# Starting the projections of a segment-recurrent transformer earlier: halved first Q weights, second x chunk by the ACT queue, roots on ScalarE, warm-up matmuls and interleaved transposes

## The chip, the cores and the metric

The kernel runs on one core of one Trainium2 chip. The metric is the device time of one execution in microseconds (us). Most executions of this kernel lie within 0.3% of each other; here that is about 2.6 us.

## The reference

Only the first half matters here. A layer-normed x of 2048 rows by 512 is cut into 64 segments of 32 rows. Each segment is joined with 8 rows of memory that the segment before it computed; 32 heads of 128 attend over these 40 rows, and the output projection gives the next memory. So the segments are a chain. A gated MLP follows.

```python
for s in range(n_seg):                       # 64 segments, one after the other
    xs = x[:, s*32:(s+1)*32, :]
    h = concatenate([mem, xs], axis=1)       # 8 memory rows + 32 rows
    q = einsum('btd,dhe->bhte', h, Wq)       # Wq, Wk, Wv: 512 x 32 x 128, 4 MB each
    k = einsum('btd,dhe->bhte', h, Wk)
    v = einsum('btd,dhe->bhte', h, Wv)
    p = softmax(where(mask, q @ k.T * scale, -1e9))
    o = einsum('bhte,hed->btd', p @ v, Wo)
    mem = o[:, :8]                           # feeds segment s+1
    outs.append(o[:, 8:])
# then h2 = h + gated MLP of layernorm(h)
```

## The kernel before

The kernel records operations for the five engines; a small emitter works out from the tokens that each operation reads and writes which semaphores it must wait for. Every engine then runs its own list in order. The queries, keys and values of the 32 rows of a segment do not depend on the memory. The kernel computes those of its last 8 rows (the "x chunks" below, 16 segments each) apart from the rest, and for chunks 0 and 1 ahead of the loop over segments: Q groups, then V of chunk 0, half of the K groups, V of chunk 1, the other K groups. This start is what the change touches. (`...` marks cuts.)

```python
def load_xe(ck, j):
    t, tok = xbuf(j)
    sp(lambda e: e.dma_start(t, xe[CK*ck:CK*ck+CK, XM:SEG, :]), writes=tok)
def load_w(mi, hq):                          # 8 heads of one matrix: 1 MB
    ...
    sp(lambda e: e.dma_start(ws[:, :, c0:c1], wr[:, :, c0:c1]), writes=[("W", mi, hq)])

load_xe(0, 0)                                # all on the SP queue, in order
load_xe(1, 1)
for hq in range(4): load_w(0, hq)            # Wq
...
def ln_stats(j):                             # mean and variance on VectorE, root on GpSimd
    dve(... bn_stats ...); dve(... bn_aggr ...)
    pool(... var + EPS ...); pool(... ** -0.5 ...)
def qkx_mm(ck, i, bank):                     # one group: 16 matmuls of 128x128x128
    for hh in range(4):
        for dc in range(DC):
            pe(... matmul(ps[:, bank, ...], lhsT=ws[:, dc, ...], rhs=hTe[:, ck % 3, dc, :]) ...)
...
for j in range(2): ln_stats(j)
for j in range(2):
    ln_apply(j); xT(j, 6 + j); xe_copy(j, 6 + j)     # transpose on TensorE, copy on ScalarE
for mi in (2, 1):                            # Wv, then Wk
    for hq in range(4): load_w(mi, hq)
for i in range(8):                           # Q groups, 2 of each weight quarter per chunk
    for ck in range(2): start_group(qkx_mm, qkx_evac, ck, i)
    ...
for n in range(8):                           # V of chunk 0
    ...
    start_v(0, n)
    if n == 1: xT(4, 6); ring_copy(0, 6)
    if n == 2: xT(5, 7); ring_copy(1, 7)
    if n == 3: xT(6, 6); xe_copy(2, 6); mem0_transpose(7); load_wo(0)
load_wo(1)
for j in range(2): load_vx(j)                # reads stored V back
for i in range(8, 12):                       # first K groups
    for ck in range(2): start_group(qkx_mm, qkx_evac, ck, i)
for n in range(8):                           # V of chunk 1
    start_v(1, n)
    if n % 4 == 3: load_wo(2 + n // 4)
for i in range(12, 16): ...                  # last K groups
...
for s in range(NSEG): ...                    # the loop over segments
```

The softmax here doesn't subtract the row's maximum and nothing guards it: scores larger than these inputs give would overflow.

## Time and profile before

| | us |
|---|---|
| time before, median of 3 runs (870.05 to 871.07) | 870.4 |
| span in the profile | 869.6 |
| TensorE busy | 848.4 (98%) |
| first Q matmul | 8.01 |
| first K group | 33.65 |
| first matmul of the loop over segments | 55.17 |

The page of the kernel before: its span, the busy time of the engines, and the first line of the chain of work that ended last.

```profile
span 869.6 us, 45456 instructions
...
PE 848.4 (98%) x22453; PEld 433.6 (50%) x18876; DVE 502.0 (58%) x1246; ACT 467.4 (54%) x1291; POOL 158.6 (18%) x427
...
PE 96%; DVE 2%; DMA 1%; issue 1%; ACT 0%; POOL 0%; SPq 0%; DVEq 0%
...
```

TensorE is nearly always busy and makes up 96% of that chain. A change of the start can therefore gain only what it moves the loop forward.

The timeline of the first 14 us. Columns: start in us, duration, engine, line of the source, operation, output<-input, and in brackets the idle time of the engine before it and what ended that.

```profile
...
2.16 2.67 SPq L315 DMA_DIRECT2D f_arena<-in_A_Wq_dram  x4
...
5.17 0.69 DVE L364 BATCH_NORM_STATS2 f_st<-f_xn 128x6 f32<-128x512 bf16 x1 [0.82 <-DMA f_xn<-in_A_x_dram]
...
5.99 0.38 DVE L374 TENSOR_SCALAR f_xn<-f_xn,f_mv,f_rs 128x512 bf16<-128x512 bf16 x1
...
6.43 0.61 PE L384 MATMUL f_ps<-f_ident,f_xn 128*128 128x128 bf16 x4 [6.43 <-DVE f_xn L374]
...
9.96 0.74 ACT L436 ACTIVATE f_arena<-f_ps 128x512 bf16<-128x512 f32 x1 [1.11 <-PE f_ps L426]
11.67 0.73 DVE L438 CAST f_arena<-f_ps 128x512 bf16<-128x512 f32 x1 [4.12 <-PE f_ps L426]
13.06 0.75 ACT L436 ACTIVATE f_arena<-f_ps 128x512 bf16<-128x512 f32 x1 [2.36 <-PE f_ps L426]
13.95 0.74 DVE L438 CAST f_arena<-f_ps 128x512 bf16<-128x512 f32 x1 [1.55 <-PE f_ps L426]
```

VectorE waits for the second x chunk (5.17) before it normalizes the first (5.99). After the Q matmuls begin, the evacuations of the first groups start 9.96, 11.67, 13.06, 13.95: a group of 16 matmuls takes 1.71 us at first and 0.89 us later, 107 and 56 ns per matmul. The Trainium skill ("TensorE: Matmul & The Clock Gate", Part 1) gives 106.7 and 55.6 ns for a cold and a warm array, and this trace agrees. The trace's clock record begins with an entry of 1.0 at 12.54 us; that is where the spacing changes.

TensorE alone, from the timeline: the Q groups, the V groups, the first K groups, the loop.

```profile
...
8.01 16.62 PE L426 MATMUL f_ps<-f_hTe,f_arena 128*128 128x128 bf16 x256
24.57 1.91 PE L461 MATMUL f_ps<-f_arena,f_hTe 128*32 128x512 bf16 x32
...
30.08 3.64 PE L461 MATMUL f_ps<-f_arena,f_hTe 128*32 128x512 bf16 x64
33.65 7.32 PE L426 MATMUL f_ps<-f_hTe,f_arena 128*128 128x128 bf16 x128
...
55.17 0.40 PE L280 MATMUL f_ps<-f_arena,f_hT 128*32 128x512 bf16 x4
...
```

Each load is confirmed by 16 DMA engines, and the trace has the time of each confirmation. I call the last of the 16 the landing. The first 1 MB of Wq landed at 7.76; the first piece of Wk landed at 31.79, although 14 of its engines were through by 30.63.

```profile
...
q8 instruction: 164, 2.69, 1.4%
...
```

The columns are packets, MB and share of the 16 engines. 2.69 MB in 164 packets is 16.4 KB each. TensorE runs 22,453 matmuls and 18,876 weight loads, 252 per packet. The Trainium skill ("Advanced Engine Details and Errata", ISA Cache) gives a line of 16 KB, 256 instructions; this agrees. Nearly all of this queue is TensorE's instruction stream.

### The profile page before, as it was taken

The page shows a single profiled execution, that of the slowest core. Times are in us where ns is not written, and L with a number is a line of the kernel's source. Part 1 is how long each engine was busy: PE and PEld are TensorE (multiplying, and loading weights), DVE is VectorE, ACT ScalarE, POOL GpSimd, SP SyncE. Part 2 cuts the span into 40 slices and gives each one's busy share as a digit, 9 for nine tenths or more (in the row PEclk, how much of TensorE's full clock was granted, in tenths as well). Part 3 has the DMA queues.
Part 4 walks back from the last instruction along what each step waited for, and adds up shares of the span by engine and source line. Part 5 has one row for each costly group of instructions (what it writes and reads, how often), then busy time and mean ns, then how long its engine had stood idle before and what let it go on. Part 6 is the DMA issues. An engine that isn't in the chain of part 4 may idle for free.

```text
span 869.6 us, 45456 instructions
## 1 busy us (share of the span) xinstructions
PE 848.4 (98%) x22453; PEld 433.6 (50%) x18876; DVE 502.0 (58%) x1246; ACT 467.4 (54%) x1291; POOL 158.6 (18%) x427
## 2 busy tenths in 40 slices
PE   6999999999999999999999999999999999999996
PEld 6664445554444545454454544545544444444443
DVE  3546666666666666666666666566565554454343
ACT  3445666666666666656666666666666655300000
POOL 1621212121122112121212212121111122100000
PEclk9999999999999999999999999999999999999999
DMA  9972333214041222332241313333221790033001
GB/s 319 380 218 72 72 71 74 65 41 81 29 91 33 75 39 52 76 67 62 68 85 40 79 50 83 70 80 71 47 67 38 200 267 1 0 109 110 25 19 33
DMA packets 114183, 75.23 MB, mean 87 GB/s; under 512 B 70712, under 2 KB 99520, under 8 KB 113984
## 3 DMA queue, kind: packets, MB, share of 16 engines
q1 hardware_dynamic: 113984, 72.26, 30.8%
q8 instruction: 164, 2.69, 1.4%
q14 instruction: 35, 0.29, 0.1%
HBM read 39.46 MB, written 20.58 MB: 69 GB/s over the span
## 4 chain that ended last, share of the span: by engine, by line
PE 96%; DVE 2%; DMA 1%; issue 1%; ACT 0%; POOL 0%; SPq 0%; DVEq 0%
PE f_ps L280 30%; PE f_ps L660 13%; PE f_ps L281 13%; PE f_ps L1092 11%; PE f_ps L426 3%; PE f_ps L710 3%; PE f_ps L461 3%; PE f_ps L1054 3%; PE f_ps L574 3%; PE f_ps L625 3%; PE f_ps L1085 3%; PE f_ps L1166 2%; PE f_ps L631 1%; PE f_ps L554 1%; PE f_ps L681 1%
## 5 line engine op out<-in xcount | busy, mean ns | idle before, releaser
L280 PE MATMUL f_ps<-f_arena,f_hT 128*32 128x512 bf16 (+1 forms) x5120 | 352.7, 337 | 1.6 <-issue 0.5
L281 PE MATMUL f_ps<-f_arena,f_hT 128*32 128x256 bf16 (+1 forms) x3072 | 214.4, 308 | 0.0
L280 PEld LDWEIGHTS f_ps<-f_arena,f_hT 128*32 128x32 bf16 x5120 | 121.1, 96 | 168.5 <-issue 85.2
L518 ACT ACTIVATE f_Tst<-f_ps 128x512 bf16<-128x512 f32 (+1 forms) x320 | 149.8, 510 | 57.6 <-PE f_ps L280 53.9
L660 PE MATMUL f_ps<-f_arena,f_cT 128*32 128x256 bf16 x4096 | 133.9, 273 | 1.2 <-ACT f_cT L645 1.1
L597 POOL TENSOR_TENSOR f_E_sb<-f_R_sb,f_E_sb 128x64 bf16<-128x64 f32 x128 | 48.2, 377 | 378.7 <-ACT f_R_sb L589 378.7
L526 DVE STREAM_TRANSPOSE f_QT<-f_Tst 128x256 uint32<-128x256 uint32 x128 | 57.1, 446 | 94.9 <-ACT f_Tst L518 94.9
L660 PEld LDWEIGHTS f_ps<-f_arena,f_cT 128*32 128x32 bf16 x4096 | 92.4, 95 | 34.9 <-ACT f_cT L645 21.1
L1092 PE MATMUL f_ps<-f_arena 128*128 128x512 bf16 x448 | 100.6, 379 | 0.0
L617 DVE TENSOR_SCALAR f_V_sb<-f_ps 128x512 bf16<-128x512 f32 (+1 forms) x128 | 70.6, 552 | 41.1 <-PE f_ps L280 41.1
L672 ACT ACTIVATE f_part<-f_ps 128x256 bf16<-128x256 f32 x128 | 49.2, 384 | 67.4 <-PE f_ps L660 67.4
L647 DVE TENSOR_SCALAR f_cT<-f_ps 128x160 bf16<-128x160 f32 (+1 forms) x192 | 61.0, 374 | 38.3 <-PE f_ps L631 38.3
L645 ACT ACTIVATE f_cT<-f_ps 128x160 bf16<-128x160 f32 (+1 forms) x192 | 53.0, 348 | 39.4 <-PE f_ps L631 39.4
L1092 PEld LDWEIGHTS f_ps<-f_arena 128*128 128x128 bf16 x448 | 43.8, 98 | 52.7
L526 DVE STREAM_TRANSPOSE f_KT<-f_Tst 128x128 uint32<-128x128 uint32 (+1 forms) x192 | 66.0, 356 | 2.7
L585 ACT ACTIVATE f_R_sb<-f_ps 128x160 f32<-128x160 f32 x128 | 38.9, 304 | 33.6 <-PE f_ps L281 26.4
L1098 DVE TENSOR_TENSOR f_arena<-f_ps,f_arena 128x512 f32<-128x512 f32 x28 | 19.3, 690 | 54.4 <-PE f_ps L1092 52.4
L567 ACT ACTIVATE f_E_sb<-f_ps 128x224 bf16<-128x224 f32 x128 | 45.7, 357 | 0.1
L593 DVE TENSOR_TENSOR f_E_sb<-f_R_sb,f_E_sb 128x160 bf16<-128x160 f32 x128 | 44.8, 350 | 0.0
L589 ACT ACTIVATE f_R_sb<-f_R_sb 128x160 f32<-128x160 f32 x128 | 42.6, 333 | 2.0
L710 PE MATMUL f_ps<-f_arena,f_cTx 128*32 128x512 bf16 x512 | 40.5, 380 | 0.0
L280 PE MATMUL f_ps<-f_arena,f_hTe 128*32 128x512 bf16 x512 | 39.0, 382 | 0.0
(105 smaller groups left out, 1026.0 us busy)
## 6 DMA issues: line engine op xcount, KB each, us to landing
wT_d<-f_wst SPq DMA_DIRECT2D x32, 256.0 KB, 2.9
f_arena<-wT_d SPq DMA_DIRECT2D x32, 256.0 KB, 4.2
f_arena<-in_A_Wq_dram SPq DMA_DIRECT2D x4, 1024.0 KB
f_arena<-in_A_Wv_dram SPq DMA_DIRECT2D x4, 1024.0 KB
f_arena<-in_A_Wk_dram SPq DMA_DIRECT2D x4, 1024.0 KB, 15.6
f_arena<-in_A_Wo_dram SPq DMA_DIRECT2D x4, 1024.0 KB
f_Vx<-vext_d SPq DMA_DIRECT2D x128, 32.0 KB
f_xn<-in_A_x_dram SPq DMA_DIRECT2D x16, 128.0 KB, 2.1
```

Source lines behind the costliest of these rows:

```text
L280: return e.matmul(out, lhsT=lhsT, rhs=rhs, start=start, stop=stop, skip_group_check=True, tile_position=pos)
L281: return e.add_instruction(mybir.InstMatmult(name=nc.get_next_instruction_name(), engine=mybir.EngineType.PE, ins=[e.lower_ap(rhs), e.lowe ...
L518: act(lambda e: e.activation(out=st_.rearrange("p (hp i r) -> p hp i r", i=32, r=2), in_=ps[:, bank, 0:64 * np_].rearrange("p (hp r i) -> ...
L526: dve(lambda e: e.transpose(out=dst, in_=src), reads=tok, writes=[(nm, b, k) for k in halves(b, p0, np_)])
L597: pool(lambda e: e.tensor_tensor(out=ev, in0=rv, in1=ev, op=ALU.mult), reads=[("R", b), ("Ex", b)], writes=[("Ex", b)])
L617: dve(lambda e: e.tensor_scalar(out=dst, in0=src, scalar1=VSC, scalar2=None, op0=ALU.mult), reads=[PB(bank)], writes=tok)
L645: act(lambda e: e.activation(out=dst, in_=src, func=ACT.Copy, scale=UNSC), reads=[PB(PVB[c])], writes=tok)
L647: dve(lambda e: e.tensor_scalar(out=dst, in0=src, scalar1=UNSC, scalar2=None, op0=ALU.mult), reads=[PB(PVB[c])], writes=tok)
L660: pe(lambda e, h=h, g=g, i=i, b=b, c=c: e.matmul(ps[32 * g:32 * g + 32, bank, 0:d1 - d0], lhsT=cTh[:, i, 8:40], rhs=w_o[:, h, d0:d1], star ...
L672: act(lambda e: e.activation(out=part[:, s % 8, d0:d1], in_=ps[:, bank, 0:d1 - d0], func=ACT.Copy), reads=[PB(bank)], writes=[("part", s % ...
L710: pe(lambda e, h=h, g=g, i=8 * qr + bg: e.matmul(ps[32 * g:32 * g + 32, WXB, :], lhsT=cTx[:, rb % 2, i, :], rhs=w_o[:, h, :], start=(i < 4 ...
L1092: pe(lambda e: e.matmul(ps[:, bank, 0:TB], lhsT=z2[:, sc, fb * 128:(fb + 1) * 128], rhs=wTb[tb % 2][:, :, sc, :], start=(sc == 0), stop=(s ...
```

## The change

The intent is to let TensorE begin real work earlier and at full speed. The first 8 heads of Wq come in two pieces of 4 heads; chunk 1 is issued by the ACT queue in parallel; the two roots are computed on ScalarE as exp(-0.5 ln(var + eps)); 44 matmuls on a tile of ones run while TensorE would wait; chunk 1's transposes go between the first two halves of Q; and three transposes in the V stage move one group later.

```diff
-    def load_xe(ck, j):
+    def load_xe(ck, j, q="sp"):
         t, tok = xbuf(j)
-        sp(lambda e: e.dma_start(t, xe[...]), writes=tok)
+        em.add(q, lambda e: e.dma_start(t, xe[...]), writes=tok, dma=True)
     def load_w(mi, hq):
+        if mi == 0 and hq == 0:
+            cm = c0 + 4 * DH
+            sp(lambda e, c0=c0: e.dma_start(ws[:, :, c0:cm], wr[:, :, c0:cm]), writes=["W0"])
+            c0 = cm
         sp(lambda e: e.dma_start(ws[:, :, c0:c1], wr[:, :, c0:c1]), writes=[("W", mi, hq)])
+    load_xe(1, 1, "act")
     load_xe(0, 0)
-    load_xe(1, 1)
 # ... (ln_root: bn_aggr on VectorE, then Ln and Exp on ScalarE; xe_halves: two transposes
 #      per bank, one half copied by ScalarE, the other by VectorE; qkx_mm takes a choice of
#      heads and waits for "W0" alone where the first piece suffices)
-    for j in range(2):
-        ln_stats(j)
-    for j in range(2):
-        ln_apply(j)
-        xT(j, 6 + j)
-        xe_copy(j, 6 + j)
+    for _ in range(44):
+        pe(lambda e: e.matmul(ps[:, 1, 0:128], lhsT=onesrc[:, 0:128], rhs=onesrc[:, 0:128], ...), ...)
+    ln_bn(0)
+    ln_root(0)
+    ln_bn(1)
+    ln_apply(0)
+    ln_root(1)
+    xe_halves(0, 0, (6, 7))
+    ln_apply(1)
+    for hp in range(2):
+        for i in range(2):
+            qkx_mm(0, i, 2 + i, (2 * hp, 2 * hp + 1))
+        if hp == 0:
+            xe_halves(1, 1, (0, 1))
+    # ... (evacuations of these groups, then chunk 1's groups 0 and 1)
-    for i in range(8):
+    for i in range(2, 8):
 # ... (in the V stage: n == 1, 2, 3 become n == 2, 3, 4)
```

More of the change, by code (lines that the diff above doesn't have):

```diff
@@ L305, in xbuf @@
         return (xn[:, j, :], [("xn", j)]) if j < 2 else (part[:, j, :], [("part", j, 0), ("part", j, 1)])
-    def load_xe(ck, j):
+    def load_xe(ck, j, q="sp"):
         t, tok = xbuf(j)
-        sp(lambda e: e.dma_start(t, xe[CK * ck:CK * ck + CK, XM:SEG, :]), writes=tok)
+        em.add(q, lambda e: e.dma_start(t, xe[CK * ck:CK * ck + CK, XM:SEG, :]), writes=tok, dma=True)
     def load_w(mi, hq):
@@ L314, in load_w @@
         c0, c1 = hq * 8 * DH, (hq + 1) * 8 * DH
+        if mi == 0 and hq == 0:
+            cm = c0 + 4 * DH
+            sp(lambda e, c0=c0: e.dma_start(ws[:, :, c0:cm], wr[:, :, c0:cm]), writes=["W0"])
+            em.mark_const("W0")
+            c0 = cm
         sp(lambda e: e.dma_start(ws[:, :, c0:c1], wr[:, :, c0:c1]), writes=[("W", mi, hq)])
         em.mark_const(("W", mi, hq))
+    load_xe(1, 1, "act")
     load_xe(0, 0)
-    load_xe(1, 1)
     for hq in range(4):
@@ L358, in late_consts, with ln_bn @@
         pool(lambda e: e.tensor_copy(out=mask[:, 224:448], in_=mask[:, 0:224]), reads=["mask"], writes=["mask"])
-    def ln_stats(j):
+    def ln_bn(j):
         t, tok = xbuf(j)
@@ L364, in ln_stats, with ln_root @@
         dve(lambda e: e.bn_stats(out=st1[:, k, :], in_=t), reads=tok, writes=[("st1", k)])
+    def ln_root(j):
+        k = j % 3
+        dve(lambda e: e.bn_aggr(out=mv1[:, k, :], in_=st1[:, k, :]), reads=[("st1", k)], writes=[("mv1", k)])
+        act(lambda e: e.activation(out=rs1[:, k:k + 1], in_=mv1[:, k, 1:2], func=ACT.Ln, bias=EPS), reads=[("mv1", k)], writes=[("rs1", k)])
+        act(lambda e: e.activation(out=rs1[:, k:k + 1], in_=rs1[:, k:k + 1], func=ACT.Exp, scale=-0.5), reads=[("rs1", k)], writes=[("rs1", k)])
+    def ln_stats(j):
+        k = j % 3
+        ln_bn(j)
         dve(lambda e: e.bn_aggr(out=mv1[:, k, :], in_=st1[:, k, :]), reads=[("st1", k)], writes=[("mv1", k)])
@@ L379, in ln_inplace, with xT @@
         ln_apply(j)
-    def xT(j, bank):
+    def xT(j, bank, dcs=range(DC)):
         t, tok = xbuf(j)
-        for dc in range(DC):
+        for dc in dcs:
             pe(lambda e, dc=dc: e.transpose(out=psb[:, bank, dc * 128:(dc + 1) * 128], in_=t[:, dc * 128:(dc + 1) * 128],
@@ L393, in x_flip @@
         sp(lambda e: e.dma_start(xs_d[i], t), reads=rd, writes=[("xs", i)])
-        sp(lambda e: e.dma_start_transpose(out=dst, in_=xs_d[i]), reads=[("xs", i)], writes=[tok])
+        sp(lambda e: e.dma_start_transpose(out=dst, in_=xs_d[i]), reads=[("xs", i)], writes=tok)
     def ring_fill(rb):
@@ L408, in xe_copy, with xe_halves @@
         src = psb[:, bank, 0:512].rearrange("p (dc c) -> p dc c", dc=DC)
-        act(lambda e: e.activation(out=hTe[:, ck % 3, :, :], in_=src, func=ACT.Copy), reads=[PB(bank)], writes=[("hTe", ck % 3)])
+        act(lambda e: e.activation(out=hTe[:, ck % 3, :, :], in_=src, func=ACT.Copy), reads=[PB(bank)],
+            writes=[("hTe", ck % 3, 0), ("hTe", ck % 3, 1)])
+    def xe_halves(ck, j, banks):
+        for hf in range(2):
+            xT(j, banks[hf], (2 * hf, 2 * hf + 1))
+        for hf in range(2):
+            src = psb[:, banks[hf], 256 * hf:256 * hf + 256].rearrange("p (dc c) -> p dc c", dc=2)
+            dst = hTe[:, ck, 2 * hf:2 * hf + 2, :]
+            if hf == 0:
+                act(lambda e, dst=dst, src=src: e.activation(out=dst, in_=src, func=ACT.Copy), reads=[PB(banks[0])], writes=[("hTe", ck, 0)])
+            else:
+                dve(lambda e, dst=dst, src=src: e.tensor_copy(out=dst, in_=src), reads=[PB(banks[1])], writes=[("hTe", ck, 1)])
     def mem0_transpose(bank):
@@ L417, in mem0_transpose, with qkx_mm @@
         act(lambda e: e.activation(out=hT[:, 0, :, 0:M], in_=src, func=ACT.Copy), reads=[PB(bank)], writes=[("hTm", 0, 0), ("hTm", 0, 1)])
-    def qkx_mm(ck, i, bank):
+    def qkx_mm(ck, i, bank, hhs=range(4)):
         mi, q = i // 8, i % 8
         ws = (w_q, w_k)[mi]
-        for hh in range(4):
+        for hh in hhs:
+            wt = "W0" if i < 2 and hh < 2 else ("W", mi, q // 2)
             h = 8 * (q // 2) + 2 * hh + q % 2
@@ L427, in qkx_mm @@
                                                          rhs=hTe[:, ck % 3, dc, :], start=(dc == 0), stop=(dc == DC - 1)),
-                   reads=[("hTe", ck % 3), ("W", mi, q // 2)], writes=[PB(bank)])
+                   reads=[("hTe", ck % 3, dc // 2), wt], writes=[PB(bank)])
     def qkx_evac(ck, i, bank, eng="act"):
@@ L445, in qkx_rows @@
                                           dc == 0, dc == DC - 1, (0, 32 * c)),
-               reads=[("hTe", ck % 3), ("W", mi, 2 * b), ("W", mi, 2 * b + 1)], writes=[PB(bank)])
+               reads=[("hTe", ck % 3, dc // 2), ("W", mi, 2 * b), ("W", mi, 2 * b + 1)], writes=[PB(bank)])
     def qkx_flip(ck, mi, r, b, bank):
@@ L462, in vx_mm @@
                                                        start=(dc == 0), stop=(dc == DC - 1), tile_position=(0, 32 * c)),
-                   reads=[("hTe", ck % 3), ("W", 2, n // 2)], writes=[PB(bank)])
+                   reads=[("hTe", ck % 3, dc // 2), ("W", 2, n // 2)], writes=[PB(bank)])
     def vx_evac(ck, n, bank, eng="act"):
@@ L758, in fast_path @@
     act(lambda e: e.preload_act_table_set("natural_log_exp_and_others"))
-    for j in range(2):
-        ln_stats(j)
-    for j in range(2):
-        ln_apply(j)
-        xT(j, 6 + j)
-        xe_copy(j, 6 + j)
+    for _ in range(44):
+        pe(lambda e: e.matmul(ps[:, 1, 0:128], lhsT=onesrc[:, 0:128], rhs=onesrc[:, 0:128], start=True, stop=True), reads=["onesrc"], writes=[PB(1)])
+    ln_bn(0)
[10 more added lines that the diff above has]
+            xe_halves(1, 1, (0, 1))
+    qkx_evac(0, 0, 2, "act")
+    qkx_evac(0, 1, 3, "dve")
+    for i in range(2):
+        qkx_mm(1, i, 4 + i)
+        qkx_evac(1, i, 4 + i, ("act", "dve")[i])
     for mi in (2, 1):
@@ L797, in fast_path @@
         start_v(0, n)
-        if n == 1:
+        if n == 2:
             xT(4, 6)
             ring_copy(0, 6)
-        if n == 2:
+        if n == 3:
             xT(5, 7)
             ring_copy(1, 7)
-        if n == 3:
+        if n == 4:
             xT(6, 6)
@@ L985, in fast_path @@
         if j4 == 1 and 2 <= rb + 2 < RB:
-            late.append(lambda rb=rb: (ln_apply(0), x_flip(0, rb, xn[:, 1, :].rearrange("p (dc c) -> p dc c", dc=DC), ("xn", 1))))
+            late.append(lambda rb=rb: (ln_apply(0), x_flip(0, rb, xn[:, 1, :].rearrange("p (dc c) -> p dc c", dc=DC), [("xn", 1)])))
         if s == 2:
@@ L989, in fast_path @@
         if s == 3:
-            late.append(lambda: (ln_apply(7), x_flip(7, RB, hTe[:, 0, :, :], ("hTe", 0))))
+            late.append(lambda: (ln_apply(7), x_flip(7, RB, hTe[:, 0, :, :], [("hTe", 0, 0), ("hTe", 0, 1)])))
         if j4 == 1 and rb >= 2:
```

## The prediction

> **What bounds the kernel.** The chain of waits is 96% TensorE; TensorE is busy 98% of an 869.6 us span. The loop of 64 segments, from 55.2 us on, is untouched. The change moves only the first 34 us, and everything after by that amount: a few us at most, well under 2%.
>
> **Before, from the timeline and the chain of waits (us from the start).** x chunk 0 has landed by 3.42; chunk 1, queued second, by 5.14. VectorE, in order, waits for chunk 1 until 5.17, so chunk 0's normalization (rstd ready 5.32) starts at 5.99. Transposes 6.43, copy 7.08 to 7.68, first Q matmul 8.01. The first 1 MB of Wq lands at 7.76, just in time. Evacuations of the first Q groups come 1.71 apart (107 ns per matmul), from 13 us on 0.89 (56 ns). The Trainium skill ("TensorE: Matmul & The Clock Gate", Part 1) gives these two spacings for a cold and a warm array; the trace agrees. About 40 Q matmuls run cold: 40 x 51 ns = 2.1 us. Q ends at 24.57; the V stage takes 9.08, about 0.9 of it idle or wait; the K groups start at 33.65.
>
> **The change, costed.**
> 1. Chunk 1 by the ACT queue: both chunks land by about 3.5 to 4.2; the 1.7 us wait goes.
> 2. Roots as two ScalarE operations (0.2 us each) for 0.22 + 0.57 on GpSimd. But ScalarE is in order: chunk 1's roots stand ahead of chunk 0's copy. Estimate: apply 5.2, transposes 5.7, ScalarE copy 6.3, first Q matmul 6.7: gain 1.3.
> 3. 44 matmuls on ones from about 1.2 us, 4.7 us cold: the array is warm about at the first Q matmul: gain up to 2.1.
> 4. Wq's first 1 MB in halves: the first half lands around 6 and does not gate; smaller rows cost about 0.2.
> 5. Transposes one V group later: up to 0.5 of V-stage idle.
>
> TensorE alone would gain about 3.7 us.
>
> **What takes part back.** The 16 DMA engines are saturated (share 1.05, 385 GB/s) from 4.5 to 34 us, 2.7 us per 1 MB weight piece, the last engine 1.1 behind the others. Last landings before: Wv pieces 21.0, 23.7, 26.4, 29.1; first Wk piece 31.8, used at 33.65: slack 1.9. The weight stream starts about 0.7 earlier (issue 1.5 for 2.16), less 0.2 and some ramp: first Wk piece at about 31.4. So from the V stage on TensorE becomes bound by weight arrival, and the gain is cut from 3.7 to about 33.65 - 31.4 = 2.3. The second Wk piece (34.5 before, used at 37.3) and Wo have slack, so the loop keeps 2.3.
>
> **Predicted: 868.0 us, 8 in 10 between 866.6 and 869.3.** Faster by over 2%: 0.01; within 2%: 0.98; slower by over 2%: 0.01.
>
> **What would show each step.** First Q matmul at 6.3 to 7.0; group spacing 0.89 from the start; Q done at about 21.2; TensorE idle of 0.3 to 0.7 ahead of Wv groups and the first K group, put down to weight DMAs; K groups start at 31.0 to 31.8; the loop's duration unchanged to 0.3.
>
> **What would make it wrong.** If the lagging DMA engine catches up, the gain is 3 to 3.7 (867); if the lag grows, or the ACT queue's load delays chunk 0, 1 to 1.5. If the array does not count the ones as work, 1 to 2 us of cold matmuls return, largely hidden behind the weight arrival.

## The result, and the profile after

| | before | after |
|---|---|---|
| median us | 870.74 (870.05 to 871.36, 4 runs) | 870.9 (869.87 to 871.38, 4 runs) |
| ratio | | 1.0000, 95% interval 0.9983 to 1.0018 |

A ratio is the mean time of one kernel's fast runs over the mean of the other's in the same rounds, so it is not quite the ratio of the medians. The predicted gain of 2.3 us is not there.

The page after, with the lines that answer to those of before:

```profile
span 869.6 us, 45548 instructions
...
PE 851.9 (98%) x22497; PEld 435.4 (50%) x18920; DVE 502.0 (58%) x1248; ACT 467.1 (54%) x1295; POOL 156.1 (18%) x423
...
q8 instruction: 164, 2.69, 1.3%
...
PE 93%; DMA 2%; SPq 2%; DVE 1%; issue 1%; ACT 0%; DVEq 0%
...
```

The timeline of the first 7 us after: chunk 1 is issued by ScalarE's queue, the two statistics follow each other without a wait, and chunk 0 is normalized at 5.22 instead of 5.99.

```profile
...
0.80 0.66 ACTq L309 DMA_DIRECT2D f_xn<-in_A_x_dram  x1
...
1.54 0.82 SPq L317 DMA_DIRECT2D f_arena<-in_A_Wq_dram  x1
...
3.81 0.69 DVE L369 BATCH_NORM_STATS2 f_st<-f_xn 128x6 f32<-128x512 bf16 x1 [3.81 <-DMA f_xn<-in_A_x_dram]
...
4.64 0.66 DVE L369 BATCH_NORM_STATS2 f_st<-f_xn 128x6 f32<-128x512 bf16 x1
...
5.22 0.41 DVE L389 TENSOR_SCALAR f_xn<-f_xn,f_mv,f_rs 128x512 bf16<-128x512 bf16 x1
...
6.10 0.36 ACT L434 ACTIVATE f_hTe<-f_ps 128x256 bf16<-128x256 bf16 x1
...
```

TensorE alone, with the same columns as before:

```profile
...
1.08 4.34 PE L788 MATMUL f_ps<-f_onesrc 128*128 128x128 bf16 x44 [1.08 <-POOL f_onesrc L333]
5.69 0.40 PE L399 MATMUL f_ps<-f_ident,f_xn 128*128 128x128 bf16 x4 [0.28 <-DVE f_xn L389]
6.52 1.07 PE L454 MATMUL f_ps<-f_hTe,f_arena 128*128 128x128 bf16 x16 [0.43 <-ACT f_hTe L434]
...
7.99 13.90 PE L454 MATMUL f_ps<-f_hTe,f_arena 128*128 128x128 bf16 x240 [0.18 <-DMA f_arena<-in_A_Wq_dram]
21.82 1.91 PE L489 MATMUL f_ps<-f_arena,f_hTe 128*32 128x512 bf16 x32
24.10 1.05 PE L489 MATMUL f_ps<-f_arena,f_hTe 128*32 128x512 bf16 x16 [0.37 <-DMA f_arena<-in_A_Wv_dram]
...
32.20 7.31 PE L454 MATMUL f_ps<-f_hTe,f_arena 128*128 128x128 bf16 x128 [0.89 <-DMA f_arena<-in_A_Wk_dram]
...
53.70 0.40 PE L280 MATMUL f_ps<-f_arena,f_hT 128*32 128x512 bf16 x4
...
```

The start works: matmuls on ones from 1.08, Q from 6.52 at 0.9 to 1.0 us per group (the clock record now begins at 4.70), Q done at 21.82 instead of 24.57. Then the waits for weights appear: 0.18 for Wq, 0.37 for Wv, and 0.89 us for the first piece of Wk, which landed at 32.06. The K groups begin at 32.20, 1.45 us earlier than before, not 2.3; the loop begins at 53.70 instead of 55.17. And yet both spans are 869.6 us. So two questions are open: why the start gained only 1.5 us, and where that went during the loop.

### The profile page after: what moved, and what is told of

Same layout as the page of the kernel before. It is cut to its first block, busy times and chain, and to the rows that moved or that the text cites. A ratio compares the mean times of both kernels' runs of the same rounds, so it can differ in the third digit from the quotient of the medians.

```text
span 869.6 us, 45548 instructions
## 1 busy us (share of the span) xinstructions
PE 851.9 (98%) x22497; PEld 435.4 (50%) x18920; DVE 502.0 (58%) x1248; ACT 467.1 (54%) x1295; POOL 156.1 (18%) x423
## 4 chain that ended last, share of the span: by engine, by line
PE 93%; DMA 2%; SPq 2%; DVE 1%; issue 1%; ACT 0%; DVEq 0%
PE f_ps L280 30%; PE f_ps L688 13%; PE f_ps L281 13%; PE f_ps L1133 11%; PE f_ps L738 3%; PE f_ps L1095 3%; PE f_ps L602 3%; PE f_ps L489 3%; PE f_ps L1126 3%; PE f_ps L653 3%; PE f_ps L1207 2%; PE f_ps L454 2%; DMA f_arena<-in_A_Wk_dram 2%; PE f_ps L582 1%; PE f_ps L659 1%; SPq L320 1%
```

## The experiments

Terms: "array fast at" is the first 1.0 in the clock record. "Wk landed" is the landing of Wk's first piece. A marker for the loop is ScalarE's first exponential of each segment. Each timed set has 5 rounds; the kernels of one set share a chip and the runs of the kernel before. A ratio is always to the kernel before.

My theory T at first: the start's gain is capped by weight arrival, and the loop lost the rest to TensorE stalls that fall by chance. The rival R: something systematic in the loop gives the gain back.

### Set 1: both kernels again, the order of K and V, and no warm-up

**a_again**: the changed kernel, no edit.

> The changed kernel again, unedited. Two theories of why the measured time did not fall although the loop started 1.47 us earlier. T (chance): the loop lost 1.4 us to a handful of short TensorE stalls (0.2 to 0.9 us each, put down to issue) that fall in other places in every execution; then here the first K group starts again near 32.2 us and the loop near 53.7 us, the stalls sit in other segments than before (not again at segments 33 and 46), and over more runs the ratio to the kernel before is about 0.9985 (1.3 us gained). R (systematic): something in the loop gives the gain back, e.g. a position of the instruction stream; then the stalls recur in the same segments and the ratio stays at 1.000.

**b_again**: the kernel before, no edit.

> The kernel before, unedited, as a control of the noise. T: ratio 1.000 within 0.0008, loop start near 55.2 us again, the loop's duration differs by up to 1 us from the first trace's 623.6 us and the stalls are in other places. R: the loop takes 623.6 us again within 0.3 us, with stalls in the same segments (20 and 50).

**kfirst**: all K groups ahead of V, Wk loaded ahead of Wv.

```diff
-    for mi in (2, 1):
+    for mi in (1, 2):
         for hq in range(4):
             load_w(mi, hq)
+    for i in range(8, 16):
+        for ck in range(2):
+            start_group(qkx_mm, qkx_evac, ck, i)
     for n in range(8):
         ...
         start_v(0, n)
-    for i in range(8, 12): ...      # K groups between the V stages
-    for i in range(12, 16): ...     # K groups after them
```

> The changed kernel with the K groups of chunks 0 and 1 ahead of both V stages, and Wk loaded ahead of Wv. A Q or K piece of 1 MB feeds 3.6 us of matmuls, a V piece feeds 1.8 us per chunk, and a piece takes 2.7 us to arrive: in this order TensorE should not wait for weights. If weight arrival is what cut the start's gain: no TensorE wait put down to Wk or Wv, the Q-K-V part ends and the loop starts at 51.0 to 52.0 us (53.7 in the changed kernel, 55.2 before), total about 2 us below the changed kernel. If something else holds the start (evacuations, banks): loop start stays near 53.7.

**nowarm**: the changed kernel without the matmuls on ones.

```diff
-    for _ in range(44):
-        pe(lambda e: e.matmul(ps[:, 1, 0:128], lhsT=onesrc[:, 0:128], rhs=onesrc[:, 0:128], ...), ...)
```

> The changed kernel without the 44 matmuls on ones. If weight arrival sets the start of the K groups: Q matmuls run 107 ns apart for some 4 to 6 us, Q ends about 2 us later (near 23.8), but the first K group still starts at 31.7 to 32.5 and the loop within 0.5 us of 53.7; total unchanged within 0.1%. If the warm array is what brought the start forward: K groups and loop start about 2 us later (34 and 55.7). The ones also add 88 instructions to TensorE's stream: if their extra instruction fetch is what held up the last DMA engine, Wk lands 0.3 to 1.2 us earlier here.

Measured:

| | array fast at | first K group | loop starts | median us | ratio (95%) |
|---|---|---|---|---|---|
| a_again | 4.60 | 32.59 | 54.10 | 870.36 | 0.9986 (0.9972 to 1.0000) |
| b_again | 10.36 | 32.51 | 54.03 | 870.54 | 0.9996 (0.9983 to 1.0009) |
| kfirst | 6.39 | (order differs) | 51.85 | 879.21 | 1.0085 (1.0071 to 1.0100) |
| nowarm | 11.18 | 32.47 | 53.98 | 871.98 | 1.0002 (0.9987 to 1.0017) |

The control b_again upset my baseline. TensorE of b_again:

```profile
...
7.89 15.62 PE L426 MATMUL f_ps<-f_hTe,f_arena 128*128 128x128 bf16 x256 [0.21 <-DMA f_arena<-in_A_Wq_dram]
...
32.51 7.32 PE L426 MATMUL f_ps<-f_hTe,f_arena 128*128 128x128 bf16 x128
...
```

The very same kernel began its K groups 1.14 us earlier than in the trace that I had predicted from (33.65), because its array became fast at 10.36 and not at 12.54. Part of the "gain" that I had counted was one execution's late clock.

nowarm shows that the warm array itself is hidden:

```profile
...
9.71 14.27 PE L454 MATMUL f_ps<-f_hTe,f_arena 128*128 128x128 bf16 x240
...
32.47 7.31 PE L454 MATMUL f_ps<-f_hTe,f_arena 128*128 128x128 bf16 x128
...
63.53 0.26 PE L653 MATMUL f_ps<-f_E_sb,f_V_sb 32*128 32x40 bf16 x13 [2.56 <-issue]
...
65.94 2.54 PE L688 MATMUL f_ps<-f_arena,f_cT 128*32 128x256 bf16 x44 [1.14 <-DMA f_arena<-in_A_Wo_dram]
...
```

Q is about 2 us later than in the changed kernel (TensorE leaves Q at about 23.9), yet the K groups start at 32.47, as in the changed kernel (32.20, 32.59): weight arrival (32.33 here) decides. The expectation also asked whether the instruction fetch of the ones holds up the last DMA engine: then Wk should land earlier here, and it does not. The last two lines belong to the loop's first segment: a wait of 2.56 us without a named releaser and 1.14 us for Wo. The clock record then shows 0.5 from 65.80 to 69.21, so the array cooled in the loop. These waits are one trace's; I return to them below.

kfirst removed the wait for Wk, and the loop started 2 us earlier than in the changed kernel, as expected. But the total went up by 0.85%:

```profile
...
8.66 27.93 PE L454 MATMUL f_ps<-f_hTe,f_arena 128*128 128x128 bf16 x496 [0.72 <-DMA f_arena<-in_A_Wq_dram]
...
51.85 0.39 PE L280 MATMUL f_ps<-f_arena,f_hT 128*32 128x512 bf16 x4
...
64.74 0.41 PE L688 MATMUL f_ps<-f_arena,f_cT 128*32 128x256 bf16 x4 [4.93 <-DMA f_arena<-in_A_Wo_dram]
68.71 1.69 PE L688 MATMUL f_ps<-f_arena,f_cT 128*32 128x256 bf16 x28 [3.57 <-DMA f_arena<-in_A_Wo_dram]
```

TensorE ran into Wo, the output weights: 4.93 and 3.57 us of waiting in segment 0 (and a clock record of 0.5 from 64.42 to 74.66). In this order the last two pieces of Wo were issued at 55.9 and 59.3, because SP's queue, in order, first stood at loads of V that had still to be stored. One gate was removed, and the loop, 8 us after its earlier start, ran into the next. My expectation of a 2 us gain was wrong.

On T against R: the largest extra times were in the same segments again in each kernel. I come to this after set 3, where it was tested.

### Set 2: one part of the change at a time, and Wo earlier

**b_warm**: the kernel before plus the 44 matmuls on ones alone.

```diff
+    for _ in range(44):
+        pe(lambda e: e.matmul(ps[:, 1, 0:128], lhsT=onesrc[:, 0:128], rhs=onesrc[:, 0:128], ...), ...)
     for j in range(2):
         ln_stats(j)
```

> The kernel before plus only the 44 matmuls on ones. Found so far: the array became fast at 12.54 and 10.36 us in two executions of the kernel before, at 4.7 and 4.6 us in two of the changed kernel; the first K group started at 33.65 and 32.51 against 32.20 and 32.59, because the first Wk piece had not fully landed earlier (31.8 before, 32.1 and 32.5 changed). If so, the ones alone do all that can be done: Q groups 0.89 us apart from the start, Q ends near 22.5, the first K group waits for Wk and starts at 31.8 to 32.3, loop start 53.3 to 53.8, total 0.5 to 1.2 us below the kernel before. Stalls in the loop: if they go with the position of the 16 KB instruction fetches in TensorE's stream (88 instructions later here, as in the changed kernel), they move from segments 20 and 50 to 33 and 46; if they belong to anything else in the change, they stay at 20 and 50.

**x1sp**: the changed kernel with chunk 1 on the SP queue.

```diff
-    load_xe(1, 1, "act")
     load_xe(0, 0)
+    load_xe(1, 1)
```

> The changed kernel with the second x chunk back on the SP queue, behind the first. Question: why did the weights land no earlier (first Wk piece 32.06 and 32.45, before 31.79 and 31.82) though their first issue moved from 2.16 to 1.54 us? If the second queue's packets set the 16 engines apart (first to last engine of the first Wq piece 1.1 to 2.3 us in the changed kernel, 0.5 to 0.6 before), then here the spread is 0.5 to 0.8 again and Wk lands at 31.5 to 31.9; chunk 1 lands near 5, VectorE waits for it, first Q matmul at 7.3 to 8.0, but the first K group starts at 31.6 to 32.0, not later than in the changed kernel. If the halves of Wq are to blame, the spread stays over 1 us and Wk at 32.0 to 32.5.

**nosplit**: the changed kernel with the first Q weights in one piece.

```diff
-        if mi == 0 and hq == 0:
+        if False:
-            wt = "W0" if i < 2 and hh < 2 else ("W", mi, q // 2)
+            wt = ("W", mi, q // 2)
```

> The changed kernel with the first Q weights in one piece of 1 MB again. If the halves (1 KB rows) slow the weight stream or spread the engines: first Wk piece lands at 31.4 to 31.8 and its spread falls to that of before; the first K group starts 0.4 to 0.8 us earlier than in the changed kernel (32.2, 32.6) although the first Q matmul starts later (7.5 to 7.9). If the ACT queue is to blame: Wk at 32.0 to 32.5 still, and no change of the loop's start.

**kfirst_wo**: kfirst with all of Wo issued ahead of the loads of stored V.

```diff
-    load_wo(1)
+    for hq in range(1, 4):
+        load_wo(hq)
     for j in range(2):
         load_vx(j)
     for n in range(8):
         start_v(1, n)
-        if n % 4 == 3:
-            load_wo(2 + n // 4)
```

> K ahead of V as in the run kfirst (where the loop started at 51.85 us, 2 us earlier, but TensorE then waited 8.5 us for the output weights Wo in segment 0, whose last two pieces were issued at 55.9 and 59.3, behind loads that wait for stored V), and with all four Wo pieces issued ahead of those loads. If only the order in the SP queue made Wo late: no wait for Wo, loop start near 51.9, segment 0 within 1.5 us of the changed kernel's, total 1 to 3 us below the changed kernel (867.5 to 869.5). If the 16 DMA engines simply cannot move 17 MB and the V stores before about 60 us: a wait of about 1 to 3 us for Wo, stored V, or an instruction fetch appears in segment 0 and the total is within 1 us of the changed kernel.

Measured:

| | array fast at | first Q matmul | Wk landed | first K group | loop starts | median us | ratio (95%) |
|---|---|---|---|---|---|---|---|
| b_warm | 6.29 | 8.39 | 31.82 | 31.95 | 53.46 | 870.79 | 1.0002 (0.9989 to 1.0014) |
| x1sp | 5.52 | 6.56 | 31.67 | 31.81 | 53.32 | 870.84 | 1.0000 (0.9987 to 1.0013) |
| nosplit | 4.56 | 8.71 | 31.52 | 33.11 | 54.63 | 872.22 | 1.0014 (1.0001 to 1.0026) |
| kfirst_wo | 4.09 | 6.65 | (order differs) | (order differs) | 52.33 | 869.89 | 0.9989 (0.9973 to 1.0006) |

b_warm: the ones alone bring the K groups to 31.95, as early as the whole change does. Nearly everything else in the change aims at the first Q matmul, and that is not what decides.

```profile
...
31.95 7.31 PE L426 MATMUL f_ps<-f_hTe,f_arena 128*128 128x128 bf16 x128
...
```

x1sp: chunk 1 landed at 4.10 by the SP queue (3.44 by the ACT queue in the first trace after), and the first Q matmul came at 6.56 (6.52 there). The 1.7 us wait for chunk 1 that I read from the first trace is not the rule: in the other three traces of the kernel before chunk 1 landed at 4.05 to 4.20. It is not rare either: of the eight traces with chunk 1 on the SP queue, two had it after 5 us (5.14, and 5.13 in kfirst_wo_sp below), and of the ten with the ACT queue none had it after 3.67. But chunk 0 landed 0.4 us later in those ten (3.76 to 3.91) than in the eight (3.37 to 3.49). The Trainium skill ("DMA: Bandwidth & Descriptors", Issuing engines are not separate DMA queues) says that a second issuing engine saves only the time to initiate a transfer. Here Wq's first issue was at 2.16 without the ACT queue and at 1.54 with it, and Q began no earlier; this run agrees.

nosplit: undoing the halves made the start worse. The whole piece landed at 8.57, TensorE waited 2.56 us for it, and the array cooled.

```profile
...
8.71 1.86 PE L454 MATMUL f_ps<-f_hTe,f_arena 128*128 128x128 bf16 x16 [2.56 <-DMA f_arena<-in_A_Wq_dram]
...
```

From the windows view, the columns are busy time and number of instructions of each engine, then the granted clock (PEclk):

```profile
...
core 0: us, PE busy (x) PEld busy (x) DVE busy (x) ACT busy (x) POOL busy (x), PEclk, DMA share, GB/s
...
8.00:12.00 4.00, 3.29 (x37) 3.32 (x38) 0.29 (x1) 0.66 (x2) 0.00 (x0) 0.58 1.05 401
12.00:16.00 4.00, 4.00 (x76) 4.00 (x74) 1.71 (x3) 1.95 (x3) 0.00 (x0) 1.00 1.06 370
...
```

The clock of 0.58 from 8 to 12 us comes from an entry of 0.5 from 7.97 to 11.38 in the clock record. So the halves belong to the warm-up: without them the ones are wasted. Wk landed at 31.52 here and at 31.67 in x1sp, a little earlier than in any trace of the changed kernel (32.03 to 32.65). So the halves and the second queue together may cost the weight stream a few tenths. But in kfirst and kfirst_wo, which keep both, the piece at the same place in the stream (there the first of Wv) landed at 31.41 and 31.89. With one trace each this is a hint at most, and I leave it open.

kfirst_wo: the wait for Wo is gone. The loop starts at 52.33, and segment 0 takes 1.69 us longer than in its shortest trace, with 0.77 us of waiting for stored V. The ratio, 0.9989, is near a_again's 0.9986, and its interval holds 1.

### Set 3: the reordering without the change, and the position of the instruction stream

By now all traces with the 44 ones showed extra time in segment 46 and those without them in segment 50. I formed a third theory, P: the stalls go with the position of the loop in TensorE's instruction stream. 44 matmuls and their weight loads are 88 instructions. Between segments 20 and 50 the traces record 17,963 instructions of TensorE (17,880 matmuls and weight loads, and 83 of its sequencer), 599 per segment, 2,395 for four segments; nine fetches of 256 are 2,304; 91 remain. So 88 more instructions in front should bring the same place of a segment to the same place of a fetch four segments earlier. P can be tested by adding a whole fetch.

**a_pad**: 256 added instructions instead of 88.

```diff
-    for _ in range(44):
-        pe(lambda e: e.matmul(ps[:, 1, 0:128], lhsT=onesrc[:, 0:128], rhs=onesrc[:, 0:128], ...), ...)
+    for _ in range(128):
+        pe(lambda e: e.matmul(ps[:, 1, 0:32], lhsT=onesrc[:, 0:128], rhs=onesrc[:, 0:32], ...), ...)
```

> The changed kernel with 128 matmuls of 32 columns on ones in place of 44 of 128: 256 added instructions in TensorE's stream, one whole instruction fetch of 16 KB, so that the loop lies against the fetches as in the kernel before. The extra stalls of the loop were at segments 20 and 50 in both executions of the kernel before and in nowarm (50), at 16 and 46 in the changed kernel twice, b_warm, x1sp and nosplit; four segments hold about 2396 instructions, 92 more than nine fetches, and 88 were added. If the position against the fetch decides, here 50 (and 20) have stalls of 0.4 to 0.9 us and 46 and 16 have none. If it goes with anything else in the start, 16 and 46 remain. The start itself should stay within 0.6 us of the changed kernel's.

**b_kfirst_wo**: the edits of kfirst and kfirst_wo on the kernel before.

> The reordered weights and groups of the run kfirst_wo (K ahead of V, Wo issued early; loop start 52.3 us, ratio 0.9989) on the kernel before, that is, without the studied change of the start. If the change's earlier, warm start is real but hidden by the arrival of Wk, it shows here as a difference: the array gets fast at 10 to 13 us, Q ends at 23 to 24.6, the loop starts 1.2 to 2.5 us later than in kfirst_wo (53.5 to 54.8), while changed and unchanged start differed by only 0 to 1.4 us (53.7 and 54.1 against 55.2 and 54.0) in the given order. If the start was worth nothing: loop start 52.0 to 52.8.

**kfirst_wo_sp**: the edits of kfirst_wo and x1sp together.

> kfirst_wo with the second x chunk back on the SP queue. The run x1sp showed chunk 1 landing at 4.1 us there (3.8 to 3.9 by the ACT queue) and the first Q matmul at 6.56 us, as in the changed kernel: so the ACT queue should be worth nothing. Expected: loop start 51.8 to 52.6, ratio within 0.001 of kfirst_wo's 0.9989. If the ACT queue matters, the first Q matmul is over 0.5 us later than 6.6.

**kvmix_wo**: K groups and chunk 0's V groups alternating, Wo early.

```diff
-    for mi in (2, 1):
-        for hq in range(4):
+    for hq in range(4):
+        for mi in (1, 2):
             load_w(mi, hq)
     for n in range(8):
         ...
+        if n % 2 == 0:
+            for i in range(8 + n, 10 + n):
+                for ck in range(2):
+                    start_group(qkx_mm, qkx_evac, ck, i)
         start_v(0, n)
 # ... (the later K groups are removed, and Wo is issued early, as in kfirst_wo)
```

> The changed kernel with K groups and chunk 0's V groups alternating by weight piece (Wk, Wv, Wk, Wv: 3.6 + 1.8 us of matmuls for two pieces that take 5.4 us to arrive), V of chunk 1 last, Wo issued early. Compared with kfirst_wo: V is stored earlier, so the wait for stored V in segment 0 (0.8 us there) should go. Expected: loop start 52 to 53, segment 0 without a wait for stored V or Wo, ratio 0.997 to 0.999. If weights arrive too late in this order, waits of about 1 us for Wk or Wv appear and the loop starts at 53.5 or later.

Measured:

| | array fast at | first Q matmul | loop starts | median us | ratio (95%) |
|---|---|---|---|---|---|
| a_pad | 4.86 | 6.75 | 55.22 | 871.16 | 0.9995 (0.9980 to 1.0009) |
| b_kfirst_wo | 10.24 | 7.85 | 52.99 | 873.14 | 1.0016 (1.0001 to 1.0031) |
| kfirst_wo_sp | 6.60 | 7.61 | 52.20 | 871.51 | 1.0000 (0.9986 to 1.0013) |
| kvmix_wo | 4.67 | 6.92 | 52.01 | 871.02 | 0.9987 (0.9973 to 1.0001) |

Extra time of a segment is its duration less the shortest duration of the same segment in any of the 18 traces, in us:

| traces | added instructions | segment 46 | segment 50 |
|---|---|---|---|
| before, b_again, b_again2, b_again3 | 0 | 0.12, 0.02, 0.00, 0.03 | 0.93, 0.65, 0.92, 0.89 |
| nowarm, b_kfirst_wo | 0 | 0.00, 0.00 | 0.91, 0.90 |
| a_pad | 256 | 0.01 | 0.73 |
| after, a_again, a_again2, a_again3 | 88 | 0.77, 0.51, 1.08, 1.07 | 0.08, 0.02, 0.34, 0.43 |
| b_warm, x1sp, nosplit, kfirst | 88 | 0.58, 0.79, 1.06, 1.05 | 0.00, 0.00, 0.01, 0.00 |
| kfirst_wo, kfirst_wo_sp, kvmix_wo | 88 | 0.77, 0.77, 0.76 | 0.13, 0.11, 0.16 |

P holds in all 18 traces: with a whole fetch added the stall returned to segment 50, and the page of a_pad counts 165 instruction packets instead of 164. The time at which the loop starts does not decide: nosplit started it at 54.63 and stalled in 46, b_kfirst_wo at 52.99 and stalled in 50. The stall itself, from the chain of waits (columns: start, duration, what), in the kernel before in segment 50 and in the changed kernel in segment 46:

```profile
...
560.91 0.04 PE f_ps L681 x7
560.94 0.23 PE f_ps L280 x2
561.17 0.51 issue
561.68 0.38 PE f_ps L280 x2
...
```

```profile
...
521.11 0.04 PE f_ps L709 x7
521.15 0.23 PE f_ps L280 x3
521.38 0.56 issue
521.94 0.38 PE f_ps L280
...
```

In both it sits behind the same operations (L681 of before is L709 of after). "issue" means that TensorE waited for nothing that the profile shows. In the kernel before the instruction queue had no packet from 552.92 to 558.97, and the wait ended 2.7 us after that next packet began; in the changed kernel the packets are at 513.28 and 519.35, and the wait ended 2.6 us after the second. The packets around usually begin 3.5 to 5.4 us apart. A late instruction fetch is thus the likely cause.

A count over all 18 traces supports this. Number the instructions that a trace records for TensorE, its sequencer's included, from the start. After the first 10 us the traces hold 73 stalls of more than 0.15 us that the profile puts down to issue. Every one of them ends after 193 to 195 instructions of a block of 256, and 2.2 to 3.3 us after an instruction packet began; the 2.56 us of nowarm is one of them. Stalls with another cause would not all fall on the same place in 256. So these stalls belong to the fetches. Why one fetch is late and most are not is not shown.

But P does not explain where the loop's time went. a_pad has the stalls of the kernel before, and its time outside segment 0 is no better than the changed kernel's: summed over segments 1 to 62, the extra time is 3.4 to 3.9 us in the four traces of the kernel before, 4.0 to 4.6 in those of the changed kernel, 4.4 in a_pad, 3.5 in kfirst_wo_sp. The stall at 46 or 50 moves; it does not grow. On T against R, then: T was wrong that the largest stall falls by chance. That the ratio stays at 1.000, as R has it, is not shown either; set 4 returns to it.

a_pad missed in another way: its loop started at 55.22, not within 0.6 us of the changed kernel.

```profile
...
9.65 13.68 PE L454 MATMUL f_ps<-f_hTe,f_arena 128*128 128x128 bf16 x240 [1.62 <-DMA f_arena<-in_A_Wq_dram]
...
33.70 7.31 PE L454 MATMUL f_ps<-f_hTe,f_arena 128*128 128x128 bf16 x128 [0.85 <-DMA f_arena<-in_A_Wk_dram]
...
```

The weights are late: Wk landed at 33.57, 4.0 us after its first engine was through (2.2 to 2.7 in the changed kernel, 1.6 to 2.0 before). a_pad consumed instructions faster, and its first instruction packet of 16 KB ran at 6.68 us (12.02 in the changed kernel, 17.72 before), with more at 16.36 and 23.18; each took 0.9 to 1.2 us. That the packets set the last engine back is plausible from this, but the trace does not name the engine of a packet. b_warm, which also had three such packets before Wk, landed at 31.82, and nowarm, where only two had ended before it, at 32.33. Open.

b_kfirst_wo: with the gate at Wk gone, changed and unchanged start differ by 0.66 us at the loop's start (52.33 and 52.20 against 52.99), less than the 1.2 to 2.5 us that I expected. The changed start is itself held by the first pieces of Wq: in kfirst_wo TensorE waited 1.14 us for the second half, which landed at 9.04. The total of b_kfirst_wo is higher than that of the kernel before (1.0016): segment 0 took 2.66 us longer than its shortest, of which 1.4 us are a wait for stored V and 1.0 us a stall put down to issue.

kfirst_wo_sp is not told apart from kfirst_wo: loop start 52.20 and 52.33, and the ratios' intervals overlap (0.9986 to 1.0013 and 0.9973 to 1.0006), though its first Q matmul was a us later (7.61). The expectation had named "over 0.5 us later than 6.6" as the sign that the ACT queue matters. Chunk 1 landed at 5.13 in this trace and moved chunk 0's normalization to 5.76, but the wait that ended last was for Wq's first half (7.48), so the one trace does not tell. kvmix_wo waited 1.7 us for stored V in segment 0, against my expectation. None of the reordered versions is shown to beat both kernels. kfirst, kfirst_wo, b_kfirst_wo and kvmix_wo paid for the earlier loop in segment 0 (extra time 11.02, 1.69, 2.66 and 2.22 us). kfirst_wo_sp did not in its trace (0.62, and 0.36 to 0.65 in the four of the changed kernel), which at 868.48 was its fastest execution; its median is still 871.51.

### Set 4: four traces of each kernel

**a_again2**, **a_again3**: the changed kernel; **b_again2**, **b_again3**: the kernel before; no edits.

> The changed kernel, a third trace. Expected from two: array fast at 4 to 7 us, first K group held by the first Wk piece, starting at 31.9 to 32.7, loop start 53.4 to 54.2, stalls over 0.4 us at segments 46 and mostly 33, ratio 0.998 to 1.000. If the start were worth the 2.3 us that were predicted, the loop would start before 53.0.

> The kernel before, a third trace. Open: is the start of 55.2 us (array fast at 12.54) or that of 54.0 (array fast at 10.36) the usual one? If the moment at which the array becomes fast is a matter of chance, it lies anywhere from about 10 to 13.5 us and the loop start follows it with half the difference: 53.8 to 55.5. Stalls at segments 20 and 50. Ratio 1.000 within 0.001.

> The changed kernel, a fourth trace: as a_again2. The loop start should stay in a narrow band (53.4 to 54.2), since the arrival of Wk and not the array's clock sets it.

> The kernel before, a fourth trace: as b_again2. Over four traces each, the mean loop start before minus changed should be 0.4 to 1.2 us, and the mean ratio of the changed kernel's times about 0.9992.

| | array fast at | first Q matmul | Q done | Wk landed | first K group | loop starts |
|---|---|---|---|---|---|---|
| before | 12.54 | 8.01 | 24.57 | 31.79 | 33.65 | 55.17 |
| b_again | 10.36 | 7.89 | 23.44 | 31.82 | 32.51 | 54.03 |
| b_again2 | 11.73 | 8.06 | 24.18 | 31.86 | 33.26 | 54.78 |
| b_again3 | 13.74 | 8.29 | 25.25 | 31.66 | 34.33 | 55.85 |
| mean | 12.09 | 8.06 | 24.36 | 31.78 | 33.44 | 54.96 |
| after | 4.70 | 6.52 | 21.82 | 32.06 | 32.20 | 53.70 |
| a_again | 4.60 | 7.05 | 22.07 | 32.45 | 32.59 | 54.10 |
| a_again2 | 6.72 | 7.15 | 22.09 | 32.03 | 32.17 | 53.68 |
| a_again3 | 4.58 | 7.07 | 22.08 | 32.65 | 32.78 | 54.29 |
| mean | 5.15 | 6.95 | 22.02 | 32.30 | 32.44 | 53.94 |

The timed ratios were 0.9994 (0.9980 to 1.0007) for a_again2 and 1.0000 (0.9987 to 1.0014) for a_again3; the controls gave 1.0000 and 1.0005. The mean ratio of the changed kernel over its four timed sets (1.0000, 0.9986, 0.9994, 1.0000) is 0.9995, about 0.4 us, and no interval excludes 1. Taken together, as an estimate from the four intervals, that is 0.4 us give or take 0.6: the predicted 2.3 us are excluded, 1.0 us is not.

In every trace of the changed kernel the first K group starts 0.13 to 0.14 us after Wk's landing. In those of the kernel before it starts 0.7 to 2.7 us after it, and follows the moment at which the array becomes fast: a later clock by 3.38 us (10.36 to 13.74) delays the K groups by 1.82 us. So on average the change moves the loop forward by 54.96 - 53.94 = 1.02 us, and the kernel before is in its best case as early as the changed one.

Where that 1.02 us goes: measured from marker to marker, the loop from segment 0 to 63 took 623.58, 624.18, 624.11 and 623.73 us before (mean 623.90) and 625.01, 624.18, 625.16 and 624.96 after (mean 624.83), 0.93 us more. The part behind it took 186.29 us before and 186.79 after, on average. So in these eight traces the loop and the rest give back more than the start gains. Stalls put down to "issue" after 64 us sum to 1.08, 0.59, 1.35 and 0.69 us before and 1.77, 2.64, 0.97 and 0.87 after; that is 0.6 us of 1.4 on average, with large scatter. The rest is spread over many segments in pieces of 0.1 to 0.3 us. I could not settle its cause.

One caution changes how far this carries: the traced executions of the changed kernel were long ones for it. They took 871.23 to 871.41 us, on average 871.34, and its other 16 timed executions 870.41. The four traced executions of the kernel before averaged 871.02, and the other 12 of b_again, b_again2 and b_again3 870.99. The 0.9 us by which the four lie above the rest of their kernel is as large as the 0.93 us that their loop took longer. So it is not shown that the usual execution of the changed kernel gives back what its start gains.

## Why the prediction was wrong

- **"The change moves only the first 34 us", a few us at most, within 2%.** Right in size. That the loop is untouched was not: its stalls moved (last point).
- **Step 1, "the 1.7 us wait goes".** The wait was one of four traces': chunk 1 landed at 5.14 there and at 4.05 to 4.20 in the other three. And it cost Q little, because Q waited for Wq (next point). x1sp shows no gain from the ACT queue; whether it helps where chunk 1 would be late is not shown.
- **Step 2, first Q matmul at 6.7, gain 1.3.** Measured mean 6.95 against 8.06: 1.1 us. The chain of x went as costed, with apply at 5.22 and ScalarE's copy at 6.10 (5.2 and 6.3 predicted). But in the kernel before, the first Q matmul came 0.14 us after the landing of Wq's first piece in three traces (7.75, 7.92, 8.15) and 0.25 after it in the first (7.76). So an earlier x alone could gain at most 0.1 us there. nosplit, which has all but the halves, starts Q at 8.71.
- **Step 4, "the first half ... does not gate".** Wrong in three of four traces: TensorE waited 0.78 to 1.00 us for Wq before its first Q matmul. nosplit shows that the halves still matter, since with the whole piece TensorE waits 2.56 us and cools.
- **Step 3, the array is warm.** Right: fast at 4.58 to 6.72 us. But what this saves is a matter of chance, because the kernel before becomes fast anywhere from 10.36 to 13.74. Q was done at 22.02 instead of 24.36 on average, 2.3 us, where I had said 3.4.
- **Step 5, "up to 0.5 of V-stage idle".** Right: a wait of 0.47 to 0.48 us before the first of these transposes is in all four traces of the kernel before and in none of the changed kernel. It too is hidden by Wk.
- **"What takes part back": weight arrival.** Right as a mechanism: the wait for Wk is in all four traces, and kfirst, which removes it, starts the loop 2 us earlier. nowarm shows that the warm array is hidden by it.
- **The term that was mis-sized: "first Wk piece at about 31.4".** It landed at 32.30 on average, 0.9 us later, and 0.5 us later than before, although its stream was issued 0.6 us sooner (first issue 1.54 instead of 2.16). The first engine was through at 29.85 on average instead of 29.95; the last one fell further behind. Added to this, the baseline of 33.65 was 0.2 above the mean and a matmul starts 0.14 after the landing: 2.25 - 0.90 - 0.21 - 0.14 = 1.00 us, which is what the four traces show (33.44 - 32.44). The prediction had named this case ("if the lag grows [...] 1 to 1.5"). Why the last engine is later is open; the halves, the second queue and the instruction packets are candidates, each with a run that speaks against it (kfirst, nowarm).
- **The step that failed: "so the loop keeps 2.3", "the loop's duration unchanged to 0.3".** The loop started 1.02 us earlier on average, not 2.3, as just worked out. After that, in the traces, the loop took 0.93 us and the rest 0.50 us longer, so nothing is left in the spans; but those four executions were long ones for their kernel (set 4). The timed sets leave 0.4 us, told apart neither from zero nor from 1.0. Shown: extra times of 0.5 to 1.1 us move with the position of TensorE's instruction stream against its fetches. Not shown: why the sum grew in the traces, and whether it does in the usual execution.

## What to carry to other kernels

When weights stream in behind the matmuls, a faster start only reaches the next weight sooner: write down the landing of every piece and its first use, take the smallest slack as the most a start can gain, and look for the next gate behind it before reordering, because here the one removed (Wk) exposed others (Wo, stored V) in the first segment of the loop. A start time read from one trace is one draw; where a clock's ramp is part of it, take several traces before costing a change of one or two us, and compare the times of the traced executions with those of the others. And instructions added in front shift a long unrolled stream against its fetches, so stalls can appear in places that the change never touched.

## What the Trainium skill lacked or had wrong

- "TensorE: Matmul & The Clock Gate", Part 1, says that the moment of warming varies by 0.5 us from run to run, though it also warns that the number of cold matmuls changes between runs. Here the kernel before became fast at 10.36, 11.73, 12.54 and 13.74 us, a range of 3.38 us, with its first Q matmul at 7.89 to 8.29. That range fits the page's own free-running window of 3.4 us better than its 0.5 us.
- The same page puts the cooling at one idle window of about 3.4 us and asks for no gaps over about 3 us. Here less idle time was enough: in the 3.41 us up to the drop, TensorE was busy for 1.18 us in nosplit (4.56 to 7.97, four transposes among it) and for 1.27 us in nowarm (62.39 to 65.80). In a_pad 1.67 us of busy time from 4.86 to 8.27 kept the clock up. The slow stretches lasted 3.41 us in nosplit (7.97 to 11.38) and in nowarm (65.80 to 69.21), which agrees with the window.
- "Advanced Engine Details and Errata", ISA Cache, gives the line of 256 instructions, and the trace agrees (252 per packet). No page gives a size for what a late line costs an unrolled stream, or the place where it shows. Here it was extra time of 0.5 to 1.1 us in segment 46 or 50 that moved four segments with 88 added instructions and back with 256, and all 73 stalls over 0.15 us put down to issue ended after 193 to 195 instructions of a block of 256.
- "DMA: Bandwidth & Descriptors", Queues, rings and completion order, states that the runtime's own rows share the engines with a kernel's loads, but gives no cost. Here most 16 KB instruction packets took 1.05 to 1.1 us while weights streamed at about 385 GB/s. Whether it delays a load's last engine is open.
